# Merging short filler products at the start of a TensorE-bound kernel

## The chip, the cores and the metric

The kernel runs on one core of one Trainium2 chip. The metric is the device time in microseconds (us) of one execution; the profile's "span" is the time from the first to the last instruction and is 1.7 to 2.0 us shorter than that (in some runs of the kernel before, up to 2.8). Runs are marked fast or slow; only fast runs are compared.

## The reference

The input `x` has 2048 rows of 640 bf16 numbers. A gate mixes two branches over the same rows: linear attention with 32 heads, and an MLP block with layer norms, shifts and two skip connections.

```
g = sigmoid((x * gate_w).sum(-1))
a = linear_attention(x @ wqkv) @ wo      # phi(q), phi(k), kv = phi(k)^T v, o = phi(q) kv / den
b = x1 + gelu(layernorm(x1) @ w3) @ w4   # x1 = x + shifted(gelu(layernorm(x) @ w1)) @ w2
out = g * a + (1 - g) * b
```

Only the start matters here: the kernel computes k = x @ wk first, in 16 chunks of 128 rows, then q.

## The kernel before

The weights of k arrive as five slices of 160 KB (`wk_sb`), issued on two queues; the transposed chunks of x (`xT`) come from transposing loads that SP issues after them. Chunk 0 is different: its rows are loaded as they are (`x_sb`) and transposed on TensorE, to start sooner.

```python
    load_x(0, 1)
    aq.dma_start(g5[:], gate_w.rearrange("(c p) -> c p", p=P))
    load_wk(sp, 1)
    load_wk(aq, 0)
    load_wk(aq, 2)
    load_wk(sp, 3)
    load_wk(aq, 4)
    for c0, c1 in ((1, 2), (2, 3), (3, 4), (4, 6), (6, 8), (8, 12), (12, 16)):
        load_xT(c0, c1)
    # [cut: further loads, constants]
    def k_mm(pt, c, dcs, hfs=(0, 1), last=DC - 1):
        for dc in dcs:
            for hf in hfs:
                n = HD + hf                      # 320 or 321 columns
                nc.tensor.matmul(pt[:, hf, 0:n], lhsT=xT[:, dc, c * P:(c + 1) * P],
                                 rhs=wk_sb[:, dc, hf * HD:hf * HD + n], start=(dc == 0), stop=(dc == last))
    # [cut]
    def warmup(n, w=TS):                         # filler: products of ones, nobody reads them
        for i in range(n):
            nc.tensor.matmul(warm[:, 1, 0:w], lhsT=one[:, 0:P], rhs=one[:, 0:w], start=True, stop=True)

    warmup(6)
    warmup(3, P)                                 # "group 1"
    kp = pair()
    turns = [(pair()[:, 0, :].bitcast(BF16), a, b) for a, b in ((0, 2), (2, DC))]
    tg = warm[:, 0, :].bitcast(BF16)
    for n, (ptb, a, b) in enumerate(turns):
        for dc in range(a, b):
            nc.tensor.transpose(ptb[:, (dc - a) * P:(dc - a + 1) * P], x_sb[:, 0, dc * P:(dc + 1) * P], ident[:])
        nc.vector.tensor_copy(xT[:, a:b, 0:P], ptb[:, 0:(b - a) * P].rearrange("p (c s) -> p c s", c=b - a))
        if n == 0:
            nc.tensor.transpose(tg[:, 0:DC], g5[:], ident[0:DC, 0:DC])
            nc.vector.tensor_copy(wk_sb[:, :, D], tg[:, 0:DC])
    warmup(3, P)                                 # "group 2"
    for dc in range(DC):
        k_mm(kp, 0, (dc,))
        if dc < DC - 1:
            warmup(1, 2 * P)
    k_evac(kp, 0)
    for c in range(1, NCH):
        pt = pair()
        k_mm(pt, c, range(DC))
        k_evac(pt, c)
    # [cut: q starts here]
```

The fillers keep TensorE active while the first loads are on their way. The Trainium skill, "TensorE: Matmul & The Clock Gate", Part 1 (section "What's actually happening"), says why one would: the array starts throttled at 1.2 GHz, and sustained activity releases it to 2.4 GHz. The traces here agree with the two rates: 128 columns take 107 ns from start to start at first and 54 to 60 ns later.

## Time and profile before

| | before |
|---|---|
| time, first three runs, median (lowest to highest) | 266.99 us (266.32 to 267.23) |
| span of the profiled run | 265.1 us |
| TensorE busy | 259.4 us, 98% |
| first filler starts | 0.83 us |
| third slice of `wk_sb` lands / its product starts | 5.71 / 5.75 us |
| first product of q starts | 27.46 us |

The page of the kernel before gives the busy time of each engine (PE is TensorE's matmuls, PEld its weight loads, with instruction counts after the x), and the shares of the chain that ended last:

```profile
span 265.1 us, 4244 instructions
...
PE 259.4 (98%) x1728; PEld 162.0 (61%) x1744; DVE 139.3 (53%) x270; ACT 84.2 (32%) x122; POOL 20.3 (8%) x55
...
PE 95%; DMA 1%; ACT 1%; issue 0%; ACTq 0%; DVE 0%
```

So TensorE bounds the kernel as a whole. That says nothing about the stretch that the change touches. For it, the chain of waits of the kernel before, cut to the first 28 us; columns are start, duration, and what the chain runs through (L190 is the line of the products of k, L202 that of the fillers, L211 and L214 the transposes):

```profile
...
1.78 3.93 DMA wk_sb<-in_A_wqkv_dram
5.71 0.04 issue
5.75 0.43 PE pp L190 x2
...
6.67 9.87 PE pp L190 x72
16.54 0.01 issue
16.54 11.07 PE pp L190 x80
```

Read it from below: the first stage is TensorE work back to 5.75 us, and before that a load, the third slice of `wk_sb`, from its issue at 1.78 to its landing at 5.71. No filler before 5.75 is on this chain.

The timeline of PE in the kernel before, from 4.5 to 6.0 us (start, duration, then the instruction; neighbours of one kind are merged into one row, and the end of a matmul is modelled, so starts are what to compare):

```profile
4.55 0.33 PE L202 MATMUL pp<-const-bfloat16-1.0 128*128 128x128 bf16 x3
4.72 0.43 PE L190 MATMUL pp<-wk_sb,xT 128*128 128x320 bf16 x2
4.99 0.27 PE L202 MATMUL pp<-const-bfloat16-1.0 128*128 128x256 bf16 x1
5.10 0.44 PE L190 MATMUL pp<-wk_sb,xT 128*128 128x320 bf16 x2
5.38 0.27 PE L202 MATMUL pp<-const-bfloat16-1.0 128*128 128x256 bf16 x1
5.75 0.43 PE L190 MATMUL pp<-wk_sb,xT 128*128 128x320 bf16 x2
```

Group 2 is the first row: three products from 4.55, the next product at 4.72. A filler of 256 columns takes 0.11 us from start to start (4.99 to 5.10). The filler at 5.38 is followed only at 5.75, so about 0.27 us of TensorE time is free there, waiting for the load.

### The profile page before, as it was taken

Reading aid. Unit: us, or ns where it says so; the run is one execution under the profiler, and the core shown is the slowest. Engines: PE = TensorE matmul, PEld = TensorE weight load, DVE = VectorE, ACT = ScalarE, POOL = GpSimd, SP = SyncE. Lnnn points to the kernel's source line nnn. Section 1 sums busy time; section 2 is a strip of 40 time slices with the busy share of each in tenths; the row PEclk is TensorE's granted clock in tenths of the full one; section 3 lists DMA queues with packets and bytes.
Section 4 is the critical chain, followed back from the end, with each engine's and each line's share of the span. In section 5 each row is a group of like instructions: output and inputs, shape, how many; then the busy total and the mean of one; then the engine's idle time right before and its main releaser. Section 6 shows DMA issues by size and latency. Waiting matters only on the chain.

```text
span 265.1 us, 4244 instructions
## 1 busy us (share of the span) xinstructions
PE 259.4 (98%) x1728; PEld 162.0 (61%) x1744; DVE 139.3 (53%) x270; ACT 84.2 (32%) x122; POOL 20.3 (8%) x55
## 2 busy tenths in 40 slices
PE   8999999999999999999999999999999999999994
PEld 4667555788755644565666556567556567455662
DVE  1688688899858588955422364512464503122032
ACT  1555544321165636522510313430212340333100
POOL 7100010012300140001000001000001000000000
PEclk9999999999999999999999999999999999999998
DMA  7999987015663527500132000132000042000011
GB/s 195 181 212 370 377 242 298 0 40 122 127 97 64 78 51 193 205 0 2 29 70 77 25 0 2 21 78 77 25 0 2 1 99 77 25 0 2 0 62 37
DMA packets 46092, 23.61 MB, mean 89 GB/s; under 512 B 35450, under 2 KB 45434, under 8 KB 46074
## 3 DMA queue, kind: packets, MB, share of 16 engines
q1 hardware_dynamic: 45632, 22.86, 33.2%
q10 hardware_dynamic: 442, 0.49, 0.5%
q8 instruction: 13, 0.21, 0.4%
q14 instruction: 5, 0.04, 0.1%
HBM read 12.21 MB, written 2.62 MB: 56 GB/s over the span
## 4 chain that ended last, share of the span: by engine, by line
PE 95%; DMA 1%; ACT 1%; issue 0%; ACTq 0%; DVE 0%
PE pp L476 22%; PE pp L459 21%; PE pp L307 8%; PE pp L412 8%; PE pp L443 8%; PE pp L190 8%; PE pp L341 8%; PE pp L232 8%; DMA wk_sb<-in_A_wqkv_dram 1%; PE pp L464 1%; PE pp L485 1%; ACT m_sb L381 1%; PE pp L360 1%; PE pp L247 0%; PE pp L379 0%
## 5 line engine op out<-in xcount | busy, mean ns | idle before, releaser
L467 ACT ACTIVATE h<-pp 128x1024 bf16<-128x1024 f32 (+1 forms) x28 | 27.8, 992 | 102.8 <-PE pp L459 94.4
L459 PE MATMUL pp<-lnxT,w_sb 128*128 128x512 bf16 x249 | 59.8, 379 | 0.6
L476 PE MATMUL pp<-w_sb,h 128*128 128x320 bf16 x416 | 57.9, 299 | 0.0
L476 PEld LDWEIGHTS <-h 128*128 128x128 bf16 x416 | 40.0, 98 | 17.0 <-issue 1.9
L459 PEld LDWEIGHTS <-w_sb 128*128 128x128 bf16 x260 | 25.4, 98 | 26.7
L492 DVE SCALAR_TENSOR_TENSOR oc<-pp,omg,x 128x640 bf16<-128x640 f32 x15 | 12.9, 882 | 44.1 <-PE pp L485 27.1
L446 DVE SCALAR_TENSOR_TENSOR x<-pp,gate,x 128x640 f32<-128x640 f32 x16 | 13.9, 868 | 29.4 <-PE pp L443 29.4
L415 DVE TENSOR_TENSOR x<-pp,x_sb 128x640 f32<-128x640 f32 x16 | 13.1, 820 | 22.6 <-PE pp L412 22.6
L182 ACT ACTIVATE e<-pp 128x640 bf16<-128x640 f32 (+1 forms) x26 | 21.5, 826 | 9.6 <-PE pp L232 9.6
L443 PE MATMUL pp<-m_sb,pqT 128*128 128x320 bf16 x160 | 24.3, 299 | 0.0
L412 PE MATMUL pp<-w_sb,hsT 128*128 128x320 bf16 x160 | 23.9, 299 | 0.1
L190 PE MATMUL pp<-wk_sb,xT 128*128 128x320 bf16 (+1 forms) x160 | 22.7, 300 | 0.1
L307 PE MATMUL pp<-x_sb,pk 128*128 128x320 bf16 (+1 forms) x160 | 22.3, 300 | 0.0
L232 PE MATMUL pp<-xT,hsT 128*128 128x512 bf16 x98 | 21.6, 379 | 0.1
L307 PEld LDWEIGHTS <-pk 128*128 128x128 bf16 x160 | 18.8, 117 | 3.5
L412 PEld LDWEIGHTS <-hsT 128*128 128x128 bf16 x160 | 15.6, 98 | 8.2 <-issue 0.2
L443 PEld LDWEIGHTS <-pqT 128*128 128x128 bf16 x160 | 15.7, 98 | 7.7
L190 PEld LDWEIGHTS <-xT 128*128 128x128 bf16 x160 | 15.4, 98 | 6.6 <-DMA xT<-in_A_x_dram 0.6
L341 PE MATMUL pp<-lnxT,w_sb 128*128 128x512 bf16 x77 | 17.8, 379 | 0.2
L232 PEld LDWEIGHTS <-hsT 128*128 128x128 bf16 x100 | 11.8, 118 | 9.7
L277 POOL TENSOR_SCALAR rstd<-mv 128x4 f32<-128x4 f32 (+1 forms) x11 | 3.4, 312 | 156.5 <-DVE mv L283 156.5
L184 DVE SCALAR_TENSOR_TENSOR pk<-pp,e 128x640 bf16<-128x640 f32 x16 | 13.2, 824 | 1.7
(76 smaller groups left out, 189.7 us busy)
## 6 DMA issues: line engine op xcount, KB each, us to landing
out_dram<-oc SPq DMA_DIRECT2D x15, 160.0 KB, 1.8
w_sb<-in_B_w_dram SPq DMA_DIRECT2D x1, 2160.0 KB, 8.4
w_sb<-in_B_w_dram SPq DMA_DIRECT2D x1, 2080.0 KB, 10.2
x_sb<-in_A_x_dram SPq DMA_DIRECT2D x2, 640.0 KB, 10.0
x_sb<-in_A_x_dram SPq DMA_DIRECT2D x1, 1120.0 KB, 7.5
wo_sb<-in_A_wo_dram SPq DMA_DIRECT2D x6, 160.0 KB, 7.7
hsT<-in_A_wqkv_dram SPq DMA_DIRECT2D x1, 800.0 KB, 5.0
m_sb<-in_A_wqkv_dram SPq DMA_DIRECT2D x1, 800.0 KB, 11.1
```

What stands on the lines that cost most here:

```text
L182: nc.scalar.activation(ev, src, ACT.Exp)
L184: nc.vector.scalar_tensor_tensor(dst, src, 0.0, ev, op0=ALU.max, op1=ALU.add)
L190: nc.tensor.matmul(pt[:, hf, 0:n], lhsT=xT[:, dc, c * P:(c + 1) * P], rhs=wk_sb[:, dc, hf * HD:hf * HD + n], start=(dc == 0), stop=(dc == ...
L232: nc.tensor.matmul(pt[:, t % 2, :], lhsT=wq_sb[:, dc, :].rearrange("p (m j) -> p j m", j=DC)[:, j], rhs=xT[:, dc, t * TS:(t + 1) * TS], st ...
L307: nc.tensor.matmul(pt[:, hf, 0:HD + hf], lhsT=w, rhs=x_sb[:, c, hf * HD:(hf + 1) * HD + hf], start=(c == 0), stop=(c == NCH - 1))
L341: nc.tensor.matmul(pt[:, i, :], lhsT=w, rhs=lnxT[t][:, dc, :], start=(dc == 0), stop=(dc == DC - 1))
L412: nc.tensor.matmul(pt[:, hf, 0:HD], lhsT=hsT[:, fc, 2 + c * P:2 + (c + 1) * P], rhs=w2_sb[:, fc, hf * HD:(hf + 1) * HD], start=(fc == 0), ...
L443: nc.tensor.matmul(pt[:, hf, 0:HD], lhsT=pqT[:, j, c * P:(c + 1) * P], rhs=m_sb[:, j, hf * HD:(hf + 1) * HD], start=(j == 0), stop=(j == D ...
L446: nc.vector.scalar_tensor_tensor(x1, pt[:, :, 0:HD], gate[:, c:c + 1], x1, op0=ALU.mult, op1=ALU.add)
L459: nc.tensor.matmul(pt[:, k, :], lhsT=w3_sb[:, dc, fc * P:(fc + 1) * P], rhs=lnT[:, dc, :], start=(dc == 0), stop=(dc == DC - 1))
L467: nc.scalar.activation(h2[:, 2 * i * TS:2 * i * TS + n], pt[:].rearrange("p h e -> p (h e)")[:, 0:n], ACT.Gelu_apprx_tanh)
L476: nc.tensor.matmul(dst, lhsT=st[t]["h2"][:, fc * TS + cc * P:fc * TS + (cc + 1) * P], rhs=w4_sb[:, fc, a:b], start=start and fc == 0, stop ...
```

## The change

Three filler products of 128 columns become one of 384, in two places. The columns streamed are the same; four matmuls and their four weight loads are gone. The intent is fewer instructions in the head at the same covered time.

```diff
     warmup(6)
-    warmup(3, P)
+    warmup(1, 3 * P)
     kp = pair()
 # [cut]
-    warmup(3, P)
+    warmup(1, 3 * P)
     for dc in range(DC):
```

## The prediction

> **What bounds the kernel.** TensorE. The page's first part has PE busy 259.4 of 265.1 us (98%); the chain that ended last is 95% PE. From about 6.8 us on, matmuls run back to back (the windows: PE busy 4.00 of each 4 us). The head, before 6.8 us, is different: it is bound by loads. The chain of waits there: the DMA of `wk_sb` from 1.78 to 5.71, then PE from 5.75. A second landing follows: chunk 1's matmul starts at 6.83, after a weight-load gap of 0.21 us put down to the DMA of `xT`.
>
> **What the change does.** Two groups of three filler products of 128 columns become two products of 384 columns: four matmuls and four weight loads fewer, the same 768 columns.
>
> Costs from the timeline of PE in narrow windows, start to start:
> - Group 1 starts at 3.345 us; the first transpose starts at 3.665. So three 128-column products took 320 ns, 107 each; the 512-column ones before took 427: both 1.2 columns per ns. Estimate: one 384-column product takes 384/1.2 = 320 ns. Saved: 0.
> - Group 2 starts at 4.551 and the first real product at 4.723: 172 ns, 57 each, while the 320-column products take 135 ns (2.4 columns per ns, within 2 ns). Estimate: the merged one takes about 162 ns. Saved: about 10 ns.
> - The weight loads (98 to 147 ns, on PEld) run during the product before them; dropping four frees no time.
>
> **How much is critical.** Nothing, I think. Between group 2 and the matmul that waits for the DMA landing at 5.71 PE has slack: the filler of 5.375 could have been followed at about 5.48, yet the next product starts at 5.750, 0.27 us later. The 10 ns go into that wait. The loads do not depend on these products.
>
> **The clock.** The Trainium skill, "TensorE: Matmul & The Clock Gate", Part 1, says that the array starts at 1.2 GHz and is released to 2.4 GHz after about 3.4 us of sustained activity in a free-running window, a budget of time, not of matmuls. This trace agrees with the rates: 107 ns for 128 columns until 4.31 us, 55 ns from 4.55 on, 3.5 to 3.7 us after the first filler at 0.83. The change keeps the covered time the same (320 ns of filler before, an estimated 320 after), so the release should fall as before. If it fell one window later in some run, products between 4.6 and about 7.7 us would take twice as long; less the 0.3 us of slack, I estimate about 1.2 us more, 0.5%. That can also happen without the change.
>
> **Prediction.** 267.0 us, range 266.2 to 267.8 (the runs of before span 266.32 to 267.23). Faster by over 2%: 0.01; within 2%: 0.98; slower by over 2%: 0.01.
>
> **What would show each step right.** One 384-column product of about 320 ns start to start near 3.35 us, with the first transpose still near 3.67; another of about 162 ns near 4.55; the product that waits for `wk_sb` still starting just after that DMA lands (near 5.75); from 6.8 us on the same spacing. PE busy time unchanged within 0.2 us.
>
> **What would make it wrong.** A step of the clock at another time in most runs, because a long product counts differently as activity than three short ones; transposes that become ready inside a long filler waiting longer; a different landing order of the first loads. Each is worth 1.2 us at most by my estimate, still within 2%.

## The result

| | before | after |
|---|---|---|
| time, median of 6 (lowest to highest) | 267.11 us (266.32 to 267.86) | 266.93 us (266.72 to 267.30) |
| span of the profiled run | 265.1 us | 265.2 us |
| first product of q starts | 27.46 us | 27.51 us |

The ratio of after to before is 0.9996, with a 95% interval of 0.9977 to 1.0015: the same. (Ratios in this document are the mean time of one kernel's fast runs over that of the other's of the same rounds, so not quite the ratio of the medians quoted.)

The page of the kernel after:

```profile
span 265.2 us, 4252 instructions
...
PE 260.0 (98%) x1740; PEld 161.8 (61%) x1740; DVE 139.5 (53%) x270; ACT 84.2 (32%) x122; POOL 20.3 (8%) x55
...
PE 95%; DMA 2%; ACT 1%; ACTq 0%; DVE 0%; issue 0%
```

Weight loads went from 1744 to 1740, as the diff says. Matmuls seem to have *risen*, from 1728 to 1740. That is a fault of the record: before, there are 16 fewer matmuls than weight loads. The groups show where; from the table of groups of PE of the kernel before

```profile
L459 PE MATMUL pp<-lnxT,w_sb 128*128 128x512 bf16 x249 | 59.8, 379 | 0.6
L232 PE MATMUL pp<-xT,hsT 128*128 128x512 bf16 x98 | 21.6, 379 | 0.1
L341 PE MATMUL pp<-lnxT,w_sb 128*128 128x512 bf16 x77 | 17.8, 379 | 0.2
```

and of the kernel after:

```profile
L459 PE MATMUL pp<-lnxT,w_sb 128*128 128x512 bf16 x260 | 60.4, 379 | 0.0
L232 PE MATMUL pp<-xT,hsT 128*128 128x512 bf16 x100 | 21.7, 379 | 0.0
L341 PE MATMUL pp<-lnxT,w_sb 128*128 128x512 bf16 x80 | 17.9, 379 | 0.0
```

Eleven, two and three records are missing in the profile before: the 16. So the rise of 0.6 us in busy time is not work that the change added.

The chain of waits of the kernel after, first 28 us:

```profile
1.77 4.22 DMA wk_sb<-in_A_wqkv_dram
6.00 0.04 issue
6.04 0.43 PE pp L190 x2
...
6.97 20.71 PE pp L190 x152
```

The shape is the same: the third slice lands, now at 6.00, and its product starts at 6.04. There is no break at 16.5 us this time. The timeline of PE after, 4.5 to 6.4 us:

```profile
4.55 0.32 PE L202 MATMUL pp<-const-bfloat16-1.0 128*128 128x384 bf16 x1
4.82 0.43 PE L190 MATMUL pp<-wk_sb,xT 128*128 128x320 bf16 x2
5.09 0.27 PE L202 MATMUL pp<-const-bfloat16-1.0 128*128 128x256 bf16 x1
5.20 0.44 PE L190 MATMUL pp<-wk_sb,xT 128*128 128x320 bf16 x2
5.47 0.27 PE L202 MATMUL pp<-const-bfloat16-1.0 128*128 128x256 bf16 x1
6.04 0.43 PE L190 MATMUL pp<-wk_sb,xT 128*128 128x320 bf16 x2 [0.29 <-DMA wk_sb<-in_A_wqkv_dram]
```

Group 2 still starts at 4.55. The product behind it starts later than before (4.82, not 4.72), because the first slice of `wk_sb` landed at 4.78 in this run and at 4.32 in the other. Group 1 took 320 ns from start to start in both traces (3.345 to 3.665 before, 3.343 to 3.663 after).

One puzzle is left by these two profiles. The third slice's product started 0.29 us later than before, yet the span grew by only 0.1 us. Either the change moved the load and won something elsewhere, or loads land when they like and something later swallows the difference.

### The profile page after: what moved, and what is told of

It reads as the page before. It is cut to its first block, busy times and chain, and to the rows that moved or that the text cites. A ratio compares the mean times of both kernels' runs of the same rounds, so it can differ in the third digit from the quotient of the medians.

```text
span 265.2 us, 4252 instructions
## 1 busy us (share of the span) xinstructions
PE 260.0 (98%) x1740; PEld 161.8 (61%) x1740; DVE 139.5 (53%) x270; ACT 84.2 (32%) x122; POOL 20.3 (8%) x55
## 4 chain that ended last, share of the span: by engine, by line
PE 95%; DMA 2%; ACT 1%; ACTq 0%; DVE 0%; issue 0%
PE pp L476 22%; PE pp L459 21%; PE pp L307 8%; PE pp L412 8%; PE pp L443 8%; PE pp L341 8%; PE pp L232 8%; PE pp L190 8%; DMA wk_sb<-in_A_wqkv_dram 2%; PE pp L464 1%; PE pp L485 1%; ACT m_sb L381 1%; PE pp L360 1%; PE pp L247 0%; PE pp L379 0%; ACTq L127 0%
## 5 line engine op out<-in xcount | busy, mean ns | idle before, releaser
L459 PE MATMUL pp<-lnxT,w_sb 128*128 128x512 bf16 x260 | 60.4, 379 | 0.0
L459 PEld LDWEIGHTS <-w_sb 128*128 128x128 bf16 x260 | 25.4, 98 | 26.7
L183 DVE TENSOR_SCALAR e<-e 128x640 bf16<-128x640 bf16 (+1 forms) x26 | 9.6, 370 | 8.5 <-ACT e L182 6.9
```

Of the source, the lines that this page charges most:

```text
L459: nc.tensor.matmul(pt[:, k, :], lhsT=w3_sb[:, dc, fc * P:(fc + 1) * P], rhs=lnT[:, dc, :], start=(dc == 0), stop=(dc == DC - 1))
```

## The experiments

Three theories were on the table.

- **Slack** (mine): the short fillers end well before loads that TensorE waits for, so their length is worth nothing, merged or not.
- **Column**: the fillers are on the critical path, and the merge is neutral only because it keeps the columns.
- **Clock**: what the fillers are worth is decided by when the array is released to full rate.

Twelve runs were made: nine new kernels, the kernel before twice (*aa*, *aa2*) and the kernel after once more (*again*). The edits are against the kernel after, unless said otherwise. Each profile's head is in this table (us; the release is where the trace's record of a granted clock of 1.0 begins; "lands / starts" is the landing of a load and the start of the first product that needs it; the load of chunk 8 brings chunks 8 to 11):

| profile | clock release | third slice of `wk_sb` lands / starts | chunk 1 lands / starts | chunk 8 lands / starts | q starts | span |
|---|---|---|---|---|---|---|
| before | 4.32 | 5.71 / 5.75 | 6.78 / 6.83 | 16.50 / 16.54 | 27.46 | 265.09 |
| aa2 (before again) | 5.03 | 5.68 / 5.72 | 6.67 / 6.75 | 16.68 / 16.73 | 27.64 | 265.28 |
| after | 4.08 | 6.00 / 6.04 | 6.95 / 7.08 | 16.20 / 16.61 | 27.51 | 265.16 |
| again (after again) | 3.98 | 5.70 / 5.74 | 6.72 / 6.77 | 16.75 / 16.80 | 27.71 | 265.34 |
| none | 3.44 | 6.26 / 6.30 | 7.25 / 7.33 | 15.56 / 16.87 | 27.77 | 265.39 |
| late1 | 5.67 | 5.64 / 6.22 | 6.61 / 7.26 | 16.56 / 16.80 | 27.70 | 265.35 |
| late9 | 5.61 | 5.81 / 7.94 | 6.76 / 8.98 | 15.36 / 18.51 | 29.41 | 267.06 |
| fine | 3.63 | 5.84 / 5.91 | 7.03 / 7.07 | 16.73 / 16.78 | 27.69 | 265.32 |
| nofill | 9.96 | 5.53 / 5.57 | 6.52 / 7.13 | 15.97 / 18.06 | 28.96 | 266.55 |
| split | 5.71 | 5.89 / 5.93 | 6.85 / 6.96 | 14.30 / 16.50 | 27.40 | 264.96 |

Span minus start of q is 237.56 to 237.65 in every row, so whatever these kernels differ in is over when q starts, and q's start is a clock for the head that is far sharper than the times.

### aa and aa2: the kernel before against itself

> The kernel before against itself: ratio 1.000 by every theory. It gives the noise of the comparison (I expect an interval of about plus or minus 0.2%, 0.5 us) and a second profile of the same program: how far the landing of the third slice of wk_sb (5.71 us in the first profile) moves on its own.

> One more profile of the kernel before, because the last one of it fell in a slow state. Expected span 265.1 to 265.4; the product after the third slice of wk_sb starts about 0.04 us after a landing somewhere between 5.6 and 6.3 us, as the profiles of the other kernels had it; if it always lands at 5.71 in this kernel and later in the changed ones, the change moves the loads and my theory is wrong in that.

The timed runs of aa: median 267.19 us against 267.29, ratio 0.9988 (0.9968 to 1.0009). So an identical program reads 0.1% faster here; a ratio of 0.999 is no gain. The mean span of aa's fast runs is 265.20 us against 265.40 for before in the same rounds, so mean spans of identical programs can differ by 0.20 us. The profile of aa fell in a slow state and is not compared with anything; the granted clock of its one core:

```profile
core 0: 342.0 us, clock 0.756
```

aa2 (one run, 266.98 us; its span of 265.3 us and its clock are those of fast runs) gave the second usable profile of before. Its third slice lands at 5.68 us, inside the 5.6 to 6.3 expected. In both usable profiles of before that landing is near 5.7, which alone would look like the load being moved by the change; *again* settles it.

### again: the kernel after, once more

> The kernel after once more, same chip. Slack theory (the short fillers end well before a load that everything waits for): ratio 1.000 within 0.2%. Column theory (the fillers are on the path, and merging is neutral only because the columns stay the same): also 1.000. Any difference over 0.3% would need a third theory. In the profile the merged product of group 1 takes about 320 ns start to start, and the product that waits for the third slice of wk_sb starts 0.04 us after its landing.

Median 267.04 us, ratio to before 0.9988 (0.9970 to 1.0006): the same, and the same as aa's ratio. The third slice lands at 5.70, its product starts at 5.74. So the landing at 6.00 in the first profile of after was that run, not the change. But the time it won there was lost again, and the chain of waits of this profile shows where:

```profile
...
9.40 7.35 DMA xT<-in_A_x_dram
16.75 0.05 issue
16.80 11.07 PE pp L190 x80
```

The chain no longer goes through `wk_sb` at all. It ends in the transposing load of chunks 8 to 11, landing at 16.75. Back-to-back chunks take 1.3625 us, so without that wait chunk 8 would have followed chunk 5 (12.23) after three chunks, at 16.31: the wait is 0.48 us. The first profile of before has the same wait, 0.17 us long, and aa2 has it too, 0.44 us. This answers the puzzle: a late third slice means a shorter wait at chunk 8.

### none: both short groups taken out

> Both short filler groups taken out altogether (768 columns gone, 320 + 162 ns of PE). Slack theory: nothing gained, 266.9 us within 0.4; the product that waits for wk_sb still starts just after the landing. Column theory: up to 0.48 us faster (266.4), about 0.2%, with that product earlier. Clock theory: with less activity in the first window the release to full rate could come a window [...]later, which costs about 1.2 us (268.1).

```diff
     warmup(6)
-    warmup(1, 3 * P)
     kp = pair()
 # [cut]
-    warmup(1, 3 * P)
     for dc in range(DC):
```

Median 266.75 us, ratio to before 0.9977 (0.9959 to 0.9996); *again*, in the same rounds, had 0.9988. The chain of waits of this kernel:

```profile
1.78 4.48 DMA wk_sb<-in_A_wqkv_dram
6.26 0.04 issue
6.30 0.43 PE pp L190 x2
```

The transposes started at 3.34 us instead of 3.66 and the first real product at 4.39 instead of 4.82 or 4.91; then TensorE waited 1.15 us (the filler at 5.04 plus its 0.11 is 5.15; the next product starts at 6.30) for the third slice. Of 0.48 us of TensorE work removed, q's start got nothing: 27.77 against 27.71 in *again*. The column theory wanted that product earlier; it was not, though its slice landed later here (6.26) than in any other profile, so this profile alone could not show a gain. The clock theory's late release did not come either (3.44 us, the earliest of all). What the times leave open is a gain of the size 0.3 us (0.9977 against 0.9988, with overlapping intervals). The spans of all six runs say the same: their mean is 265.08 us against 265.35 for *again* and 265.40 for before, and the profiled run, at 265.4, was one of the slower ones (the others go down to 264.7). That is little more than the 0.20 us between identical programs, so it is neither shown nor excluded: in runs whose slices land early, part of the removed work could show.

### late9 and late1: more filler

> Nine more 512-column fillers ahead of the second group: at full rate 9 x 216 = 1.94 us more PE work. Slack theory: the first 0.3 to 0.5 us go into the wait for wk_sb, the rest shows: +1.4 to +1.65 us (268.4 to 268.6), and the wait for wk_sb is gone from the chain. Column theory: the whole 1.94 us shows (268.9). If the head does not matter at all: 266.9.

```diff
+    warmup(9)
     warmup(1, 3 * P)
     for dc in range(DC):
```

Median 268.74 us, ratio to before 1.0044 (1.0023 to 1.0064): clearly slower. Against *again* it is 1.70 us in medians and 1.72 us in the profiled spans (1.52 us in mean times), between my 1.4 to 1.65 (from 266.9) and the column theory's 1.94. The trace resolves it. The nine fillers start at 4.55 and end at 7.01, which is 2.46 us and not 1.94, because the first ones still ran at half rate (the release is at 5.61). So 0.74 us of 2.46 vanished. The waits of *again* add up to the same: 0.20 us at the first slice (product 4.91; group 2, at its 165 ns, is over at 4.71), 0.07 us at the third (5.74; the filler at 5.56 is over at 5.67), 0.48 us at chunk 8; together 0.75. And the chain of waits of late9 has no load left:

```profile
...
4.63 2.71 PE pp L202 x10
7.34 0.27 PE pp L190 x2
```

So the head forgives TensorE about 0.75 us of extra work in such a run, and charges the rest in full. This trace also gives the merged product at full rate with nothing waited for: 384 columns from 7.013 to 7.178, 165 ns.

> One more 512-column filler ahead of the second group: 216 ns more PE work at full rate, less than the slack seen (0.27 us before, 0.3 to 0.5 after). Slack theory: 266.9, no change; in the profile the wait for wk_sb is shorter by about 0.2 us and the product after it still starts 0.04 us after the landing. Column theory: +0.22 us (0.08%), under the resolution of the times, so the trace decides: the product would start 0.22 us later relative to the landing.

```diff
+    warmup(1)
     warmup(1, 3 * P)
     for dc in range(DC):
```

Median 267.06 us, ratio 0.9998 (0.9976 to 1.0020): no change, as expected by the slack theory, but the profile is not the picture I had drawn. The release fell at 5.67 us, so the extra filler and what follows ran at half rate, and TensorE had no wait at the third slice: it landed at 5.64, and its product started at 6.22, behind other TensorE work. The span was still 265.35, that of *again*: chunk 8, which lands at 16.56 and starts at 16.80, had no wait of its own left. The slack was used up at the later place.

### fine: the same columns in more, shorter products

> The opposite of the change: the 384 columns of each group as six products of 64 columns, same columns. Measures what merging could save at all. If one weight load per product fits inside the product[...], 64-column products are bound by the load: group 1 takes about 6 x 107 = 640 ns instead of 320, the transposes start about 0.32 us later; group 2 at full rate about 6 x 53 = 320 ns or more instead of 162. Slack theory: the total still shows nothing (266.9 within 0.4) because the product that waits for wk_sb starts after the same landing. Column theory: same columns, so no change in group durations either. If PE time there were on the path, +0.3 to +0.5 us.

```diff
-    warmup(1, 3 * P)
+    warmup(6, P // 2)      # in both places
```

Median 267.16 us, ratio 1.0004 (0.9985 to 1.0022): no change. My expectation of the groups' lengths missed. I had taken a weight load to need the 107 ns of a 128-column product at half rate. Starts in group 1 are 3.340, 3.410, 3.463, 3.516, 3.570, 3.622, and the first transpose 3.656: 53 ns each while at half rate, 316 ns in all, no longer than the merged product. At full rate, in group 2, they are 28 to 33 ns apart (4.396 to 4.554 for five), so six take about 190 ns against 165 merged. Each of those products has its own weight load:

```profile
L202 PEld LDWEIGHTS <-const-bfloat16-1.0 x22: 96/104/147, 0.8 to 6.4; 128*128 128x128 bf16 x22
```

(columns: minimum, median and maximum duration in ns, then first and last start). A load whose record lasts about 100 ns is started every 30 to 50 ns: the duration of the record is a latency, not the rate at which loads can follow each other. So merging six products of 64 columns saves nothing at half rate and about 25 ns a group at full rate, an estimate from this one group.

### nofill: no fillers at all

> No filler at all (the six 512-column ones, both short groups and the four between the first real products are gone). Slack theory says nothing about it by PE time, as all the fillers lie before loads that PE waits for; the clock decides. Clock theory: without sustained activity from 0.83 us the release comes one or two windows later, in the 7 to 11 us region, and the products until then take twice as long: +1.2 to +3 us (268.1 to 269.9). If the fillers did nothing, 266.9.

```diff
-    warmup(6)
-    warmup(1, 3 * P)
 # [cut]
-    warmup(1, 3 * P)
     for dc in range(DC):
         k_mm(kp, 0, (dc,))
-        if dc < DC - 1:
-            warmup(1, 2 * P)
```

Median 267.83 us against 266.88, ratio 1.0027 (1.0004 to 1.0049). The release came at 9.96 us, as the clock theory said, and until then 320 columns took 267 ns from start to start (6.323 to 6.590). In this profile the loss is at the low end of the 1.2 to 3 us I gave: q starts 1.25 us later than in *again*. Over all runs it is smaller, 0.7 to 1.0 us (0.27% of 267, and the difference of the medians): the six spans fall into two groups, 265.5 to 265.8 and 266.5 to 266.7, and the profiled run is of the second. Part of the half-rate work again fell into waits for loads (its chunk 8 landed at 15.97 and was not waited for). So the fillers as a whole pay, through the clock, a quarter of a percent; their shape does not.

### free_after, free_none, free_before: the loads taken out of the way

If the slack theory is right, the fillers must begin to count as soon as nothing is waited for. These three give a wrong result on purpose (relative error 0.48): the products of k read a constant and chunk 0, which are there early.

```diff
-                nc.tensor.matmul(pt[:, hf, 0:n], lhsT=xT[:, dc, c * P:(c + 1) * P],
-                                 rhs=wk_sb[:, dc, hf * HD:hf * HD + n], start=(dc == 0), stop=(dc == last))
+                nc.tensor.matmul(pt[:, hf, 0:n], lhsT=xT[:, dc, 0:P],
+                                 rhs=one[:, 0:n], start=(dc == 0), stop=(dc == last))
```

*free_none* has no short groups besides, and *free_before* has the three and three of before.

> Wrong result on purpose: the products of the first stage read a constant and the first chunk, so none of the loads of wk_sb or of the later chunks holds PE back; the fillers are as after the change. Slack theory: with the waits gone the stage starts about 4.72 us and runs at 1.36 us a chunk without a gap; the next stage starts near 27.0 us instead of 27.5 to 27.7, so 0.5 to 0.7 us faster than the kernel before if the release of the clock falls near 4 us. Column theory, in which PE was the bound already: no gain.

> The same without the two short filler groups. Slack theory: here the fillers are on the path, so taking them away must show: about 0.48 us less than with them (320 + 162 ns), next stage near 26.5 us, where the same removal in the real kernel moved the trace by nothing. If the fillers cost nothing even when nothing is waited for: no difference. A later clock release in the one profile can hide part of it; then the sum of the pieces at their own rates has to be compared.

> The same with the fillers as before the change (three and three of 128). This isolates the change with nothing to hide it: expected 10 ns slower than merged at full rate, 0 at half rate, so no difference in the time (under 0.05 us) and group 2 of about 172 ns against 162 ns start to start.

| | median | ratio to before | release | first real product | q starts | span |
|---|---|---|---|---|---|---|
| free_after | 266.94 us | 0.9993 (0.9975 to 1.0012) | 5.25 | 4.82 | 27.56 | 265.19 |
| free_none | 266.18 us | 0.9968 (0.9947 to 0.9988) | 4.55 | 4.15 | 26.86 | 264.50 |
| free_before | 267.19 us | 1.0000 (0.9978 to 1.0021) | 4.36 | 4.72 | 27.25 | 264.88 |

The chain of waits of free_after now runs through the fillers from the start:

```profile
0.83 3.04 PE pp L202 x7
3.87 0.21 PE pp L211 x2
4.08 0.12 PE pp L214
4.20 0.43 PE pp L211 x3
4.63 0.40 PE pp L202
5.03 0.45 PE pp L190 x2
```

and that of free_none, without the groups:

```profile
0.83 2.72 PE pp L202 x6
...
3.87 0.43 PE pp L210 x3
4.30 0.47 PE pp L190 x2
```

Here the same removal that got the real kernel nothing in its profile moves q's start by 0.70 us, the span by 0.69 and the median by 0.76. That is the point of the pair, and it speaks for the slack theory and against the column theory's claim on the real kernel. It is more than the 0.48 us expected, and the trace says why. The transposes start 0.32 us sooner, as computed. From the last transpose to the first real product it is 0.51 us with group 2 and 0.16 us without, a difference of 0.35: the group ran at half rate in this profile (0.27 us and not 0.32, because a first product after a pause is followed about 0.05 us early in these records: the very first filler after 0.38 us, the others after 0.43), and it first waited for a vector copy out of its own PSUM tile (PSUM is where TensorE puts its results; the copy ends at 4.50, the group starts at 4.55, the last transpose started at 4.31).

The half rate comes from the late release in *free_after* (5.25 us). *free_before*, released at 4.36, also has both groups, and its q starts 0.39 us after that of *free_none*. So by the profiles the removal is worth 0.39 to 0.70 us when nothing is waited for. Over the six runs of each, the mean spans are 265.20 (free_after), 265.40 (free_before) and 264.52 (free_none): 0.68 to 0.88 us, against 0.27 us for the same removal in the real kernel (*again* to *none*).

The free kernel as such was not 0.5 to 0.7 us faster than before, which I had expected: with fillers it is the same (0.9993). The release was late in the profile, and the products of 320 columns ran 138 ns apart instead of 136, which over 160 products is 0.28 us. Why they did was not tested.

The change alone, free_before against free_after, is unresolved by the time (1.0000 and 0.9993) as expected; in the profiles group 2 took 172 ns split at full rate and 271 ns merged at half rate, so they cannot be compared there. The nearest to clean figures are 172 ns (free_before, after a pause) and 165 ns (late9, without one).

### split: a version that could beat both

> A version that could beat both: no short filler groups, and the transposing load of chunks 8 to 11 cut in two, so that chunk 8 lands earlier. In two profiles of four (before and after, two each) PE was caught up by that landing at 16.5 to 16.8 us with 0.2 to 0.5 us of waiting. If landings of loads set the head, chunk 8 now lands near 14.5 us and nothing waits there; the next stage starts 20.65 us after chunk 1's first product, whatever that is (27.4 to 27.9); 0.3 us, perhaps 0.5, faster than the kernel before (ratio 0.998 to 0.999), which the times can hardly tell from the same. If PE time of the fillers were the bound, -0.48 us and no effect of the split.

```diff
-    for c0, c1 in ((1, 2), (2, 3), (3, 4), (4, 6), (6, 8), (8, 12), (12, 16)):
+    for c0, c1 in ((1, 2), (2, 3), (3, 4), (4, 6), (6, 8), (8, 10), (10, 12), (12, 16)):
 # [cut]
-    warmup(1, 3 * P)
     kp = pair()
 # [cut]
-    warmup(1, 3 * P)
     for dc in range(DC):
```

Median 266.59 us against 267.02, ratio 0.9978 (0.9956 to 1.0000), result correct. The chain of waits of this kernel has one long stretch of TensorE work from chunk 1 to the end of k, without the break:

```profile
1.38 3.03 DMA wk_sb<-in_A_wqkv_dram
4.41 0.04 issue
4.45 0.69 PE pp L190 x2
...
6.85 20.71 PE pp L190 x152
```

Chunk 8 landed at 14.30 us and started at 16.50 without a wait, and q started at 27.40, the earliest of all the kernels with a correct result. It did what it was made for. (The wait that it was made to remove is in three of the four profiles of before and after, not two; and q starts 20.44 us after chunk 1, not 20.65, a figure that still had the wait of 0.17 us in it.) With an identical program reading 0.9988, the gain by time is about 0.1%, or 0.3 us, and not proven. The mean spans, 264.88 against 265.31, make a gain likely, 0.43 us where identical programs differed by 0.20; as two edits were made at once, which of them gains is not shown.

## Why the prediction was right

The time was 266.93 us against 267.0 predicted, inside the range, and the change is the same within noise. The number alone proves little: a saving of about 10 ns would not show in the time even on the critical path, so it would have come out under the column theory too. The slack is tested only by the runs that remove or add work. The steps one by one:

- *"Group 1 ... Saved: 0."* Right: 320 ns in both traces, at half rate.
- *"Group 2 ... the merged one takes about 162 ns."* The duration was right (165 ns where nothing was waited for, in late9). What I said one would see, about 162 ns near 4.55 us, was wrong: in the profile after, 274 ns pass from 4.55 until the next product, because the first slice of `wk_sb` landed only at 4.78. That is a wait for a load that I had taken as landed.
- *"dropping four frees no time"* (weight loads). Right; *fine* showed it in the other direction, with 10 more loads and no loss of time.
- *"How much is critical. Nothing."* Right for the 10 ns in question, and supported by *none* (removal of both groups gains nothing in the trace), *late1* (one more filler costs nothing) and the free kernels (the same removal is worth 0.39 to 0.70 us in the profiles once the loads are out of the way). For whole groups it is not strictly nothing: *none* may gain about 0.3 us on average. The slack of 0.27 us was right for that one place and run; over the head it was 0.75 us in *again*, as *late9* confirmed by absorbing 0.74.
- *"From about 6.8 us on, matmuls run back to back."* Wrong, without effect on the number. Chunk 8 waits for its load: 0.17 us in the profile before, 0.48 us in *again*. The table of windows hid it, since the modelled ends of matmuls cover a gap of that size: PE busy 4.00 of 4.00 us. The break at 16.54 in the chain of waits had it.
- *"the product that waits for `wk_sb` still starting just after that DMA lands (near 5.75)."* The mechanism was right (0.04 us after the landing), the moment moved with the load: 6.04, and 5.74 in the second profile.
- *"PE busy time unchanged within 0.2 us."* Wrong: +0.6 us, because 16 matmul records are missing in the profile before.
- *The clock.* The claim that the covered time matters and not the number of products was not contradicted, nor tested alone: releases at 4.08 and 3.98 us merged, 4.32 and 5.03 split, 3.63 in *fine*, with no pattern by the shape of the fillers. The "about 3.4 us" taken from the skill did not hold run by run: the release came 2.6 us (*none*) to 4.9 us (*split*) after the first filler, so the 3.5 us of the profile before was one draw. My price for a release one window late, 1.2 us, is untested, as no profile has a release near 7.7 us. It looks too high: late releases near 5.7 us (*late1*, *split*) lost nothing that the span shows, and *nofill*, with a release at 9.96, more than one window late, has a span only 1.2 us over that of *again*.

What stays open: why the same loads land up to 0.8 us apart from run to run (the third slice between 5.43 and 6.26 us over the fast profiles); whether taking the short groups out is worth 0.3 us on average.

## What to carry to other kernels

Before you shorten work at the start of a kernel, look in the chain of waits for what the work is followed by: here two kinds of loads, at 5.7 and at 16.5 us, took back, in the profiled runs, whatever TensorE won before them, and closing one wait only lengthened the next. To prove that something is off the path, take the waits away and repeat the removal: it should then count in full. A start time deep in the trace (here that of q) compares two heads to hundredths of a microsecond, where times of whole runs differ by half of one or more; but it stands for the one run profiled, so set the spans of all runs beside it.

## What the Trainium skill lacked or had wrong

- "TensorE: Matmul & The Clock Gate", Part 1, "What you observe": it says the release varies by about 500 ns either way. Here the first filler starts at 0.83 us in twelve profiles (all but *nofill* and the slow one) of kernels alike in their TensorE work until 3.3 us, and the release lies between 3.44 and 5.71 us. A spread of 2.3 us is less than the page's own free-running window of about 3.4 us but far more than its 500 ns (the same part also reports 6, 11 or 14 slow matmuls for one kernel, which is nearer). Nor does a release only after about 3.4 us of sustained activity fit: in four profiles (*none*, *fine*, *again*, *after*) it came 2.6 to 3.2 us after the first filler.
- The same page, Part 2, "Back-to-back issue gap": it gives about 81 ns at 128 columns and 131 ns at 512 for a sustained stream of weight loads and matmuls. Here such streams ran at 54 to 60 ns for 128 columns (groups of three only), 136 ns for 320 and 216 to 218 ns for 512 (216 in the median of line L459 of the kernel before, five in 1.093 us in *late9*). The page's formula for an isolated gap (columns over 2.4 plus 2.5 ns: 56, 136 and 216) fits; its sustained figures do not.
- The same page, Part 2, "LDWEIGHTS (loading the stationary operand)": it gives columns over 1.2, which is 107 ns for 128. As the duration of a record that is about right (96 to 147 ns), as a bound on the rate it is not: 64-column products, each with a 128-column load, followed each other every 53 ns at half rate and about 32 ns at full rate in *fine*. (The page also describes a faster weight load, under "Weight-path perf modes"; no run here shows whether it was in use.)
- The same page, Part 1, the note on the peak-current limiter: it says that one or two busy cores never trip it, and gives 13/16 as the third state of the clock. One run of this one-core kernel had a granted clock of 0.752 from 6.5 us to 341.0 us and a span of 342.0 us; no run shows what the other cores of the chip did.
- I found no page that says that a mean granted clock can leave out the start: the record of the granted clock in these traces begins only at the release, so the head at half rate shows as full speed, and the 0.997 of the profile before comes from a drop at 263.7 us, after the last matmul has begun at 261.0.
